# A finished background bank copied ahead of the fourth exp, second norms turned in other places, fewer background products in the attention's last steps

## The chip, the cores and the metric

The kernel runs on one core of a Trainium2 chip. The metric is the device time of one execution in microseconds (us), as a median of several runs; smaller is better. The five engines are named as the profile names them: PE is TensorE's matmul, PEld its weight load, DVE is VectorE, ACT is ScalarE, POOL is GpSimd, SP is SyncE, which here issues most DMAs. PSUM, into which TensorE writes, has eight banks, numbered 0 to 7 here. A bank holds 128x512 float32 values.

## The reference

A transformer block with adaptive layer norm, batch 1, 2048 rows, width 512, 32 heads of 16, FFN width 1792, all float32:

```
sa, ca, ga, sb, cb, gb = split(silu(c) @ w_mod)        # six vectors of 512
h = layernorm(x) * (1 + ca) + sa
q, k, v = heads(h @ wqkv)
o = softmax(q k^T / 4) v                                # 32 heads, 2048 x 2048 scores each
x = x + ga * (o @ wo)
h = layernorm(x) * (1 + cb) + sb                        # the second norm
x = x + gb * (gelu(h @ w1 + b1) @ w2 + b2)
```

The result must be near float32 accuracy. The kernel therefore splits most operands into a high and a low part and makes three products of each pair (high by high, low by high, high by low).

## The kernel before

**Blocks and units.** The rows are cut into four blocks of 512. A unit is one block of queries with four heads; there are 4x8 = 32 units, and 16 chunks of 128 keys in each, so 512 half-steps (`for hs in range(NU * NKC): half_step(hs)`). I call them steps, as the prediction does.

**What a step does** (`half_step`, L1026). For one unit and one chunk of keys: four score products `e` (`exp_mm`), each followed by an exp on ScalarE that writes a tile `p`; four products `mx` (`mx_mm`), whose row maxima VectorE takes for a unit that comes later (`LEAD` = 88 products ahead); and at its end the sums `pv` (`pv_step`) of the step before, four heads side by side. Score and maximum products use 64 of the array's rows each, so two of them on different row halves run together. PSUM is dealt out in rings: `e` has banks 0, 1, 2; `mx` has 3, 4, 5; `pv` has 6; `bg` has 7 alone.

**Background work.** Everything else of the model runs in the gaps of the steps: the projections of q, k, v, the attention's output product, the FFN. The generator `work()` yields jobs in order. A job is either a group (a list of products into one bank, and an `evac` that copies the finished bank out), a callable, or `None` (nothing to do yet). A step takes at most one new job and issues six products (`RUN = 6`) of the running group. These are cut to 64 rows as well, one half of the rows in even steps and the other in odd ones, so each pairs with an `e` or `mx` product on the other half. A group of 12 products is 24 such halves, four steps. When the group is complete, `bg_mm` calls `evac`, which puts a copy from bank 7 on ScalarE's queue. When the row halves change within a group, the first product waits for an instruction of another engine that proves the half before done; this is what the tiny copy `tick` (L1080) is for.

**The order inside a step.** With background work running, the step issues one `e` and one `mx`, then in the loop over `k` = 0 to 5 one background product and one `e` (`k` = 0, 2, 4) or `mx` (`k` = 1, 3, 5). Each exp follows its `e` at once in the order of issue, so the fourth exp (`k` = 4) stands on ScalarE ahead of the copy of a bank that gets complete at `k` = 5. Without background work the loop at the end of `half_step` issues pairs of `e` and `mx`, four times.

**The clock of the hooks.** Every exp calls `advance()`, which counts `clock["t"]` up by one and runs what was put there with `later(n, f)`. A step is four ticks. The two parts of the FFN's gelu, additions, statistics and stores are placed so. `sides` is a list of callables; each step runs one of them at its beginning. V's turns go there (`turn_v("mx")`, in a bank of the `mx` ring).

**The second norm** (`front`, L805). For a block `b`, four groups make the output product; each is copied (`y`), added to `x2[t]` on GpSimd, its statistics are taken on VectorE (`stat`), then the factor (`factor`), then the normalized rows `xn[t]` (`norm`, L818). When all four are there and nine ticks have gone by, four callables `trans(fc)` are yielded. Each takes the `bg` bank, transposes four 128x128 pieces of `xn` into it (L853), copies it out on ScalarE with scale and offset (`h`, L855), and GpSimd makes the high and the low part from it (L856, L857). A callable makes the step *full*: it runs at the step's beginning, and if the next job is a callable too, that one is held for the next step, so four steps have a turn and no background product. Blocks 1 and 2 start `front` ahead of the last part of the FFN of the block before (`"last"` in `work`), and their turns follow that part.

**The FFN** (`feed`, L863). `ffn1(i)` is a group of the first matrix; its `evac` starts the gelu: a copy `h` (L882), three GpSimd operations (L883 to L885), and with `later(10, second)` the tanh on ScalarE (L888) and four more GpSimd operations (L890 to L893). The second matrix follows in three parts (`PARTS`).

**The attention's end.** When all maxima are taken (from step 490 on), `ending` is set: the `e` ring gets banks 0 to 4, `bg` gets 5 and 7, and new groups run with all 128 rows, `RUN // 2` = 3 products in a step (`bg_whole`), behind that step's four `e` products. After the last step the running group is finished, `over[0]` is set, and the tail does what is left: from then on the gelu is one instruction (L875, L877, L878) and VectorE adds the FFN's sums. `o_prep` fetches the last unit's sums from DRAM, takes the reciprocal of the denominators (`dn`, L717), stores and loads it (`rden`, `rb`) and divides; its hooks also ask for weights (`wload`, L784). Then come the last block's output products (tile `o`), norm and FFN.

Of the kernel before, what the change touches and what calls it, by code (L numbers as in the profile page):

```python
# [23 lines left out]
KC = D // P  # L24
# [35 lines left out]
RUN = 6  # L60
# [9 lines left out]
def block_kernel(ctx: ExitStack, tc: tile.TileContext, x, wqkv, wo, w1, b1, w2, b2, c, w_mod, out):  # L70
# [179 lines left out]
    def later(n, f):  # L250
        if n:
            hooks.setdefault(clock["t"] + n, []).append(f)
        else:
            f()
# [550 lines left out]
    def front(b, x2):  # L805


        later(9, lambda: load_x2(b, x2))
        yield from until(lambda: done[b] == KC - 1)
        yield from wait(4)  # L810
        yield from loaded(b, *[("o", k) for k in range(KC)])
        mv = small.tile([P, 4, 2], F32, tag="mv", name="mv")
        rs = {}
        xn = {}

        def norm(t):
            xn[t] = tmp("xn")
            (gp if t < 3 else ve).tensor_scalar(  # L818
                xn[t], x2[t], mv[:, t, 0:1], rs[t], op0=ALU.subtract, op1=ALU.mult)
            later(40, lambda: gp.tensor_tensor(x2[t], x2[t], b2_b, op=ALU.add))  # L820

        def stat(t):
            ln_stat(mv, t, x2[t])
            later(2 if t < 3 else 1, lambda: factor(t))

        def factor(t):
            rs[t] = small.tile([P, 1], F32, tag=f"rt{t}", name=f"rt{t}")
            ve.tensor_scalar(rs[t], mv[:, t, 1:2], EPS, None, op0=ALU.add)  # L828
            gp.tensor_tensor(rs[t], rs[t], mhalf[:, 0:1], op=ALU.pow)
            later(3 if t < 3 else 2, lambda: norm(t))  # L830

        for t in range(4):

            def evac(ps, t=t):
                y = tmp("y")
                ac.activation(y, ps, AF.Copy)

                def add():
                    gp.tensor_tensor(x2[t], y, x2[t], op=ALU.add)
                    later(4 if t < 3 else 3, lambda: stat(t))  # L840

                later(2, add)

            yield o_terms(b, t, range(KC)), "bg", evac
        drop(b, *[("o", k) for k in range(KC)])
        t0 = clock["t"]
        yield "ln"
        yield from until(lambda: len(xn) == 4 and clock["t"] >= t0 + 9)

        def trans(fc):  # L850
            ps = take("bg")
            for t in range(4):
                te.transpose(ps[:, t * P : (t + 1) * P], xn[t][:, fc * P : (fc + 1) * P], ident)  # L853
            h = tmp("h32")
            ac.activation(h, ps, AF.Identity, scale=modc[:, 1, fc, 0:1], bias=modc[:, 1, fc, 1:2])  # L855
            gp.tensor_copy(pc(b, fc, 0), h)  # L856
            gp.tensor_tensor(pc(b, fc, 1), h, pc(b, fc, 0).bitcast(F32), op=ALU.subtract)  # L857

        for fc in range(KC):
            yield lambda fc=fc: trans(fc)  # L860
        yield from wait(4)

    def feed(b, x2):  # L863
# [7 lines left out]
        def ffn1(i):  # L871
            def evac(ps):
                h = tmp("h")
                if over[0]:
                    ac.activation(h, ps, AF.Gelu_apprx_tanh, bias=b1_f[0][:, i : i + 1])  # L875
                    g = piece(i)
                    ac.activation(g[:, 0], h, AF.Copy)  # L877
                    ve.tensor_tensor(g[:, 1], h, g[:, 0].bitcast(F32), op=ALU.subtract)  # L878
                    gt[i] = g, clock["t"] - 9
                    return  # L880
                s = tmp("s")
                ac.activation(h, ps, AF.Identity, scale=0.5, bias=b1_h[:, i : i + 1])  # L882
                gp.tensor_tensor(s, h, h, op=ALU.mult)  # L883
                gp.tensor_scalar(s, s, GELU_C, 1.0, op0=ALU.mult, op1=ALU.add)
                gp.tensor_tensor(s, s, h, op=ALU.mult)  # L885

                def second():
                    ac.activation(s, s, AF.Tanh, scale=2 * GELU_A)  # L888
                    g = piece(i)
                    gp.tensor_scalar(s, s, 1.0, None, op0=ALU.add)  # L890
                    gp.tensor_tensor(h, s, h, op=ALU.mult)
                    gp.tensor_copy(g[:, 0], h)
                    gp.tensor_tensor(g[:, 1], h, g[:, 0].bitcast(F32), op=ALU.subtract)  # L893
                    gt[i] = g, clock["t"]

                later(10, second)

            wi = wt[b, 1, i].rearrange("p a (k n) -> p a k n", n=P)
            k = range(KC)
            return terms3([wi[:, 0, j] for j in k], [wi[:, 1, j] for j in k],  # L900
                          [pc(b, j, 0) for j in k], [pc(b, j, 1) for j in k]), "bg", evac
# [124 lines left out]
    def half_step(hs):  # L1026
# [6 lines left out]
            wload()  # L1033
        if sides:
            sides.pop(0)()
        full = False
        if act["g"] is None:
            j = held.pop() if held else next(jobs, None)
            if callable(j):
                j()  # L1040
                full = True
                j = next(jobs, None)
            if callable(j):
                held.append(j)
            elif j is not None:
                act["g"] = {"group": j, "at": [0, 0], "n": 0, "seen": None, "whole": bool(ending)}
# [7 lines left out]
            return sum(ec) < ne and ec[a] < 2 * NU * NKC  # L1054

        more = act["g"] is not None
        free = not more and not full and not ending
        if more and act["g"]["whole"]:
            while sum(ec) < ne:
                for f in [exp_mm(a) for a in range(2) if e_ok(a)]:  # L1060
                    f()
            for _ in range(RUN // 2):
                if act["g"]:
                    bg_whole()
            more = False
        k = 0
        first = more and x_ok(1 - h) and e_ok(h)
        if first:
            for f in [exp_mm(h), mx_mm(1 - h)]:
                f()  # L1070
        while more and k < RUN:
            a = 1 - h
            more = bg_mm(h)
            if first:
                if e_ok(a) and (k % 2 == 0 if x_ok(a) else sum(ec) < ne - 1 or k == RUN - 1):
                    exp_mm(a)()
                elif x_ok(a):
                    f = mx_mm(a)
                    if more and k == RUN - 1:
                        saw(ve.tensor_copy(tick, mxb[0][:, :1]))  # L1080
                    f()
            elif e_ok(a) and (sum(ec) < ne - 1 and k % 2 == 1 or not x_ok(a) and (sum(ec) < ne - 1 or k == RUN - 1)):
                exp_mm(a)()
            elif x_ok(a):
                mx_mm(a)()
            k += 1
        while sum(ec) < ne or sum(xc) < nx:
            a = 0 if ec[0] <= ec[1] else 1
            fs = []
# [7 lines left out]
                fs += [mx_mm(i) for i in range(2) if x_ok(i)]  # L1097
            for f in fs:
                f()
        if hs:  # L1100
            assert min(ec) >= 2 * cur["pv"] + 2
            pv_step()

# [162 lines left out]
```

## Time and profile before

| what | value | where it is from |
|---|---|---|
| median of 3 runs | 1719.15 us (1718.91 to 1720.06) | the times |
| profiled execution, its own time | 1721.25 us | its result |
| span of the profiled execution | 1719.5 us, 32477 instructions | head of the page |
| granted TensorE clock | 0.996 of full speed | its result |
| steps: first and last `pv` | 113.4 and 1595.7 us | the row of L669 |
| DMA | 251.89 MB, mean 146 GB/s | part 2 of the page |

The profile holds one execution. The rows of its page and of the answers to queries name the source line (L644 is line 644), the engine, the operation, and the tiles as out<-in, with buffer numbers left out. A group's row gives busy time, the mean duration of one instruction, and the idle time of its engine ahead of it with what ended most of it. A timeline row gives start, length and the instruction; in brackets stands the idle time of the engine before it and what ended it. Matmul ends are modelled, so "PE busy" is not TensorE at its peak, and a wait of a few tenths can hide in it; the time from one matmul's start to the next one's is the better measure.

### The profile page before, as it was taken

To read this page: it belongs to the slowest core of one execution; us is meant where nothing else is said; L and a number is where in the kernel's file an instruction comes from. 1 tells how busy PE (TensorE), PEld (TensorE's weight loads), DVE (VectorE), ACT (ScalarE), POOL (GpSimd) and SP (SyncE) were. 2 spreads that over 40 slices of the span, in tenths; PEclk is the share of its full clock that TensorE was granted. 3 is DMA by queue.
4 is the path that set the end of the run, shared out by engine and by line. 5 is a ranking of instruction groups with operands and counts; after the bars stand their busy time and mean duration, and the time that the engine had idled before them with its cause. 6 is when DMAs were issued, how large, how long until landed. Compare 5 with 4: busy or idle time off the path is not lost.

```text
span 1719.5 us, 32477 instructions
## 1 busy us (share of the span) xinstructions
PE 1692.2 (98%) x12073; PEld 916.6 (53%) x12073; DVE 1400.8 (81%) x2661; ACT 1238.0 (72%) x2379; POOL 694.7 (40%) x703
## 2 busy tenths in 40 slices
PE   7999999999999999999999999999999999999999
PEld 6655555555554455555555455555555545553677
DVE  7998888888889888888989888888899888870332
ACT  3357878778777778778877788778877778878231
POOL 7324444435112356415623246415633246526310
PEclk8999999999999999999999999999999999999999
DMA  8646766767447533425453444345363354423554
GB/s 292 195 156 208 221 200 204 221 192 218 125 149 210 127 99 101 104 71 153 128 163 95 111 123 119 95 107 139 116 181 82 100 143 119 98 73 116 193 156 161
DMA packets 137129, 251.89 MB, mean 146 GB/s; under 512 B 25854, under 2 KB 45324, under 8 KB 136972
## 3 DMA queue, kind: packets, MB, share of 16 engines
q1 hardware_dynamic: 135712, 248.19, 50.2%
q8 instruction: 96, 1.57, 0.4%
q10 hardware_dynamic: 1260, 1.63, 0.3%
q14 instruction: 61, 0.50, 0.1%
HBM read 188.49 MB, written 61.28 MB: 145 GB/s over the span
## 4 chain that ended last, share of the span: by engine, by line
PE 88%; DVE 6%; DMA 3%; ACT 2%; issue 0%; POOL 0%; SPq 0%; ACTq 0%; DVEq 0%; POOLq 0%
PE bg L275 39%; PE pv L669 28%; PE e L639 15%; DVE mxp L394 4%; PE mx L389 3%; DMA w<-w1s 1%; ACT p L644 1%; DVE bst L236 1%; PE pr L275 1%; PE o L275 1%; DMA wt<-wos 0%; DMA wm<-in_w_mod_dram 0%; ACT h L855 0%; PE bg L853 0%; PE mx L334 0%
## 5 line engine op out<-in xcount | busy, mean ns | idle before, releaser
L394 DVE TENSOR_REDUCE mxp<-mx 128x1 f32<-128x512 f32 x2048 | 1294.0, 683 | 163.1 <-PE mx L389 155.3
L644 ACT ACTIVATE p<-e 128x512 f32<-128x512 f32 x2035 | 1057.6, 604 | 283.5 <-PE mx L389 262.4
L389 PE MATMUL mx<-kh,qst 48*128 48x512 f32 x2048 | 835.5, 422 | 2.3 <-DVE rt L828 0.6
L639 PE MATMUL e<-qst,kh 50*128 50x512 f32 x2035 | 777.1, 429 | 6.2 <-ACT p L644 6.2
L639 PEld LDWEIGHTS e<-qst,kh 50*128 50x128 f32 x2035 | 341.6, 185 | 426.1 <-ACT p L644 218.0
L669 PE MATMUL pv<-p,vg 128*32 128x512 f32 x4096 | 546.0, 605 | 0.0
L389 PEld LDWEIGHTS mx<-kh,qst 48*128 48x128 f32 x2048 | 369.4, 185 | 19.5 <-DVE mxp L394 14.1
L275 PE MATMUL bg<-w,g 64*128 64x512 f32 (+1 forms) x1056 | 267.5, 392 | 0.8 <-DVE tick L1080 0.8
L275 PEld LDWEIGHTS bg<-w,g 64*128 64x128 f32 (+1 forms) x1056 | 193.2, 185 | 36.2 <-ACT p L644 2.7
L669 PEld LDWEIGHTS pv<-p,vg 128*32 128x32 f32 x4096 | 80.9, 108 | 177.2 <-issue 165.1
L275 PE MATMUL bg<-pchi,w 64*128 64x512 f32 (+1 forms) x624 | 174.7, 398 | 0.0
L275 PE MATMUL bg<-hThi,wqkv 64*128 64x512 f32 x560 | 155.3, 396 | 0.2 <-DVE tick L1080 0.2
L275 PEld LDWEIGHTS bg<-pchi,w 64*128 64x128 f32 (+1 forms) x624 | 111.7, 185 | 26.4 <-ACT h L882 6.1
L890 POOL TENSOR_SCALAR s<-s 128x512 f32<-128x512 f32 x41 | 61.3, 1496 | 129.1 <-ACT s L888 129.0
L275 PEld LDWEIGHTS bg<-hThi,wqkv 64*128 64x128 f32 x560 | 101.1, 185 | 16.1 <-DVE tick L1080 0.5
L909 POOL TENSOR_TENSOR x<-y,x 128x512 f32<-128x512 f32 x28 | 36.1, 1288 | 148.9 <-ACT y L908 148.4
L275 PE MATMUL bg<-pclo,w 64*128 64x512 f32 (+1 forms) x312 | 85.0, 389 | 0.0
L878 DVE TENSOR_TENSOR g<-h,g 128x512 fp32r<-128x512 f32 x15 | 10.8, 723 | 83.6 <-ACT g L877 83.6
L275 PE MATMUL bg<-hTlo,wqkv 64*128 64x512 f32 x280 | 76.5, 392 | 0.0
L275 PEld LDWEIGHTS bg<-pclo,w 64*128 64x128 f32 (+1 forms) x312 | 57.1, 184 | 10.1 <-issue 2.1
L275 PE MATMUL bg<-wo,pchi 64*128 64x512 f32 x192 | 61.2, 398 | 1.3 <-DVE tick L1080 0.6
L883 POOL TENSOR_TENSOR s<-h 128x512 f32<-128x512 f32 x41 | 42.7, 1042 | 48.4 <-ACT h L882 48.4
(159 smaller groups left out, 1366.0 us busy)
## 6 DMA issues: line engine op xcount, KB each, us to landing
kh<-qk SPq DMA_DIRECT2D x256, 192.0 KB
w<-w1s SPq DMA_DIRECT2D x56, 512.0 KB
w<-w2s SPq DMA_DIRECT2D x54, 512.0 KB
vg<-v SPq DMA_DIRECT2D x64, 332.0 KB
qk<-parts SPq DMA_DIRECT2D x32, 512.0 KB
qst<-qk SPq DMA_DIRECT2D x64, 192.0 KB
qk<-parts SPq DMA_DIRECT2D x32, 256.0 KB
ou<-osb SPq DMA_DIRECT2D x32, 256.0 KB
```

The source lines that it names most:

```text
L236: ve.bn_stats(st, rows)
L275: return te.matmul(ps, term[0][r], term[1][r], start=i == 0, stop=i == n - 1)
L389: te.matmul(ps, qst[u][r0 : r0 + KR, p, qc * P : (qc + 1) * P], kh(u, kr // 2)[r0 : r0 + KR, p, (kr % 2) * TB : (kr % 2 + 1) * TB], start= ...
L394: ins = ve.tensor_reduce(mxp[u][:, hc, kr : kr + 1], ps, axis=AX.X, op=ALU.max, negate=True)
L639: te.matmul(ps, kh(u, kc // 8)[r0 : r0 + KX, p, (kc % 8) * P : (kc % 8 + 1) * P], qst[u][r0 : r0 + KX, p], start=True, stop=True)
L644: saw(ac.activation(t, ps, AF.Exp, scale=SCALE))
L669: te.matmul(cur["ps"][32 * j : 32 * (j + 1)], vg[u][:, kc, j * VW : j * VW + 32], pt.pop(4 * s + j), start=kc == 0, stop=kc == NKC - 1)
L878: ve.tensor_tensor(g[:, 1], h, g[:, 0].bitcast(F32), op=ALU.subtract)
L883: gp.tensor_tensor(s, h, h, op=ALU.mult)
L890: gp.tensor_scalar(s, s, 1.0, None, op0=ALU.add)
L909: later(4, lambda: gp.tensor_tensor(x2[t], y, x2[t], op=ALU.add))
```

## The change

Four things are edited.

1. In a step with background work, the `e` product at `k` = 4 is issued as before, but its exp is kept in `fourth` and issued only after the loop, behind a copy that `evac` may have issued at `k` = 5. The count of the clock moves with it. `later(10, second)` becomes `later(9, second)`.
2. In blocks 1 and 2 the second norm's turns are no longer jobs. When the fourth `xn` is there, nine ticks later four callables are put into `sides`, with a bank of the `mx` ring; each runs at the beginning of a step, ahead of that step's usual work. `front` ends when all four are done and eight ticks have passed.
3. In block 0 the turns are still jobs, but a step holds its callable in `turn` and runs it after the third of its four `e` products, where there is no background group; where there is one, at the beginning.
4. In the attention's last steps a step issues two background products where `hs % 3` is not zero, and three where it is.

```diff
@@ front: norm
             later(40, lambda: gp.tensor_tensor(x2[t], x2[t], b2_b, op=ALU.add))
+            if b and len(xn) == 4:
+                later(9, lambda: sides.extend([lambda fc=fc: trans(fc, "mx") for fc in range(KC)]))
...
         t0 = clock["t"]
-        yield "ln"
-        yield from until(lambda: len(xn) == 4 and clock["t"] >= t0 + 9)
-
-        def trans(fc):
-            ps = take("bg")
+
+        def trans(fc, bk="bg"):
+            ps = take(bk)
...
             gp.tensor_tensor(pc(b, fc, 1), h, pc(b, fc, 0).bitcast(F32), op=ALU.subtract)
-
+            turned[fc] = clock["t"]
+
+        turned = {}
+        yield "ln"
+        if b:
+            yield from until(lambda: len(turned) == KC and clock["t"] >= turned[KC - 1] + 8)
+            return
+        yield from until(lambda: len(xn) == 4 and clock["t"] >= t0 + 9)
         for fc in range(KC):
             yield lambda fc=fc: trans(fc)
@@ feed: ffn1
-                later(10, second)
+                later(9, second)
@@ half_step
-        full = False
+        full, turn = False, None
         if act["g"] is None:
             j = held.pop() if held else next(jobs, None)
             if callable(j):
-                j()
+                turn = j
                 full = True
                 j = next(jobs, None)
...
         more = act["g"] is not None
+        if more and turn:
+            turn()
+            turn = None
         free = not more and not full and not ending
...
-            for _ in range(RUN // 2):
+            for _ in range(2 if hs % 3 else 3):
                 if act["g"]:
                     bg_whole()
...
         first = more and x_ok(1 - h) and e_ok(h)
+        fourth = None
...
                 if e_ok(a) and (k % 2 == 0 if x_ok(a) else sum(ec) < ne - 1 or k == RUN - 1):
-                    exp_mm(a)()
+                    if k == RUN - 2:
+                        fourth = exp_mm(a)
+                    else:
+                        exp_mm(a)()
...
             k += 1
+        if fourth:
+            fourth()
         while sum(ec) < ne or sum(xc) < nx:
...
             for f in fs:
                 f()
+            if turn and sum(ec) == ne - 1:
+                turn()
+                turn = None
         if hs:
+            assert not turn
```

## The prediction

> **What bounds the kernel now.** I read the page first (busy shares, then the chain that ended last), then cut the middle of the run into half-steps: the time from one group of attention products (`pv`) to the next, 512 in all, called steps here.
>
> ```profile
> PE 1692.2 (98%) x12073; PEld 916.6 (53%) x12073; DVE 1400.8 (81%) x2661; ACT 1238.0 (72%) x2379; POOL 694.7 (40%) x703
> ...
> PE 88%; DVE 6%; DMA 3%; ACT 2%; issue 0%; POOL 0%; SPq 0%; ACTq 0%; DVEq 0%; POOLq 0%
> ```
>
> TensorE works almost always and is 88% of the chain, so each step's length is TensorE's, plus what makes its next product wait. The next rows are stages (from:to, length, then busy us and instructions of PE, PEld, DVE, ACT, POOL): the first and second step of a background group of the first FFN matrix, the first step of an attention-output group, and the third step of such a group.
>
> ```profile
> 685.88:688.86 2.98, 2.98 (x25) 1.43 (x23) 2.62 (x6) 2.78 (x6) 2.83 (x4) 1.00 0.60 177
> 688.86:691.70 2.84, 2.84 (x24) 1.49 (x22) 2.43 (x6) 1.93 (x5) 2.38 (x3) 1.00 0.60 137
> 898.36:901.26 2.90, 2.90 (x24) 1.46 (x22) 2.54 (x6) 2.61 (x6) 1.29 (x1) 1.00 0.69 247
> 904.11:907.31 3.20, 3.12 (x24) 1.58 (x23) 3.17 (x9) 2.78 (x7) 1.55 (x2) 1.00 0.19 70
> ```
>
> An undisturbed step takes 2.84. A group's first step takes 0.14 more in the FFN case and 0.06 in the other. The timeline at such a border shows why.
>
> ```profile
> 673.03 2.07 ACT L644 ACTIVATE p<-e 128x512 f32<-128x512 f32 x4 [0.27 <-PE mx L389]
> ...
> 673.97 0.39 PE L275 MATMUL bg<-pclo,w 64*128 64x512 f32 x1
> ...
> 674.34 1.07 PE L669 MATMUL pv<-p,vg 128*32 128x512 f32 x8
> 674.81 0.61 POOL L892 CAST g<-h 128x512 fp32r<-128x512 f32 x1
> 674.96 0.71 ACT L882 ACTIVATE h<-bg,b_h 128x512 f32<-128x512 f32 x1
> ...
> 675.72 0.18 PEld L275 LDWEIGHTS bg<-pchi,w 64*128 64x128 f32 x1 [0.20 <-ACT h L882]
> ...
> 676.07 0.19 PEld L639 LDWEIGHTS e<-qst,kh 50*128 50x128 f32 x1
> ```
>
> The group's last product is done at 673.97+0.39 = 674.36, but ScalarE's copy `h` of the only background bank (7) begins at 674.96, behind four exps (2.07/4 = 0.52 each). The next group's first weight load waits 0.20 for that copy, and what follows on TensorE slips.
>
> **The change, part by part.**
>
> (a) *Copy ahead of the fourth exp.* The order of ScalarE alone changes; no instruction is added. Three exps end at 673.03+3×0.52 = 674.58, after the last product (674.36), so the copy need not wait for TensorE: it would run from 674.58 to 675.29, 0.43 before the load that waits until 675.72. Behind it on ScalarE stands the fourth exp, 675.29 to 675.81. Two things wait for that: the `pv` of the next step, 2.84 later, and the `e` bank that the next step's third score product takes (three banks in turn), whose load is at 676.07 here and about 0.14 earlier, 675.93, in an undelayed step. So the exp is covered by 0.12. How often it counts: ScalarE's copies out of that bank in the main loop.
>
> ```profile
> L882 ACT ACTIVATE h<-bg,b_h x36: 712/712/717, 617.4 to 1477.0; 128x512 f32<-128x512 f32 x36
> L908 ACT ACTIVATE y<-bg x27: 628/628/629, 715.4 to 1528.5; 128x512 f32<-128x512 f32 x27
> L309 ACT ACTIVATE pf<-bg x23: 628/628/688, 119.8 to 519.7; 128x512 f32<-128x512 f32 x23
> L644 ACT ACTIVATE p<-bg x13: 616/616/628, 522.1 to 1276.3; 128x512 f32<-128x512 f32 x13
> L323 ACT ACTIVATE vr<-bg x12: 628/628/673, 131.3 to 380.8; 128x512 f32<-128x512 f32 x12
> L836 ACT ACTIVATE y<-bg x12: 628/628/641, 547.6 to 1324.0; 128x512 f32<-128x512 f32 x12
> L855 ACT ACTIVATE h<-bg,modc x12: 777/778/779, 593.1 to 1382.5; 128x512 f32<-128x512 f32 x12
> ```
>
> 36 borders with the long copy at 0.14 = 5.0; the 74 others (27+23+12+12, all 0.628 long) at 0.06 = 4.4. Together **-9.4**; bounds 0 (the exp's cover is used up and gives it back) and -10.5. The clock of the hooks counts exps, so everything timed from a copy now comes one tick earlier. The tanh, with `later(9)` in place of 10, is issued behind the fourth exp of the second step, where ScalarE is at 1.93 of 2.84; I cost it at nothing. Uncovered (were GpSimd late with its input) it would hold the next exps. The second norm's statistics on VectorE also move a tick: they stand in the twelve 3.20 steps (DVE 3.17), 0.36 over. I take 0; if the earlier place hides them -4.3, if it doubles them +4.3.
>
> (b, c) *Turns.* The rows: a step that only turns (block 0), a step with neither turn nor background, a step with background and a turn of V beside it, and the first two of block 1's four turn steps.
>
> ```profile
> 601.85:605.35 3.50, 2.99 (x22) 1.25 (x20) 2.48 (x5) 2.73 (x7) 1.90 (x3) 1.00 0.00 0
> 881.27:884.01 2.74, 2.64 (x18) 1.01 (x17) 2.38 (x5) 2.46 (x6) 0.49 (x1) 1.00 0.98 236
> 173.04:176.59 3.55, 3.55 (x29) 1.93 (x27) 2.65 (x6) 2.60 (x7) 0.00 (x0) 1.00 0.23 59
> 980.42:984.22 3.80, 3.06 (x22) 1.25 (x20) 2.97 (x8) 2.99 (x7) 1.28 (x4) 1.00 0.20 44
> 984.22:987.72 3.50, 2.97 (x23) 1.26 (x21) 2.48 (x5) 2.73 (x7) 3.12 (x4) 1.00 0.83 204
> ```
>
> (b) Block 0: its four turns go from the head of an otherwise empty step to a place behind the third exp. At the head TensorE idles 3.50-2.99 = 0.51, since the exps wait behind the norm's copy (0.78). Behind the third exp that copy delays only the fourth. What TensorE needs: a full step less the three pairs that six background products make, at 0.23 each (the `o` row below: 9.82/42), plus a turn, 3.55-2.84 = 0.71, so 2.84-0.70+0.71 = 2.85; ScalarE needs 2.73, VectorE 2.48. I take 2.90: 4×(3.50-2.90) = **-2.4**; bounds -3.0 (2.74, all in slack) and 0. GpSimd's cast and subtract (1.90) come along, under 2.90. No DMA moves with a turn.
>
> The Trainium skill, TensorEngine Tiling (Array Packing), section Tiling Modes, says that changing the tiling mode drains TensorE. Inside the step the 128-row turn stands between 64-row pairs, so it adds one switch that the head position did not have. The row nearest to a switch is the border above: from the last product (673.97) to `pv` (674.34) are 0.37 where pairs follow at 0.23, so 0.14 by estimate, and (b) would be -1.8; the trace agrees as far as that goes.
>
> (c) Blocks 1 and 2: the eight turns go into steps that also carry background, as V's do, in a maximum bank instead of bank 7. From V's 3.55, plus 0.15 because the norm's copy is one of 0.78 ahead of four exps: 3.70 each. Eight such steps are 29.6; the eight that they replace were 2×(3.80+3×3.50) = 28.6. So **+1.0** in the loop (bounds 0 and +6.8, 4.43 each with the price doubled), but the eight now carry 48 half products, 24 whole ones, two groups, that are no longer left for the end.
>
> (d) *The end.*
>
> ```profile
> 1568.03:1570.58 2.55, 2.55 (x17) 0.94 (x16) 0.00 (x0) 2.06 (x5) 2.38 (x4) 1.00 0.39 153
> 1549.97:1593.80 43.83, 43.83 (x256) 16.47 (x255) 0.00 (x0) 39.24 (x78) 28.79 (x27) 1.00 0.31 102
> 1596.30:1617.15 20.85, 19.45 (x81) 14.82 (x81) 5.79 (x10) 4.41 (x6) 10.64 (x11) 1.00 0.58 198
> ```
>
> When the maxima are used up, 19 steps carry three whole products each: 57. Seventeen of them take 43.83, 2.58 each, with TensorE full. Groups start at step 493 as before (eight turn steps are two whole groups), and 493 mod 3 is 1, so a group of 12 now takes 2, 2, 3, 2, 2 and 1: six steps, 2.0 on average, 38 products in 19 steps. One product less is 0.23, so 2.35; ScalarE needs 39.24/17 = 2.31 with a copy and a tanh every fourth step, less with one every sixth. I take 2.37: 19×(2.58-2.37) = **-4.0**, bounds -1 and -4.4.
>
> (e) *The tail.* From the copy of the last attention bank (1596.30) to the dense output products it is 20.85. The chain there:
>
> ```profile
> 1604.01 0.06 DVE g L878
> 1604.07 0.55 issue
> 1604.61 0.36 DVE dn L717
> ...
> 1608.54 8.57 DMA wt<-wos
> 1617.11 0.04 issue
> 1617.15 9.82 PE o L275 x42
> ```
>
> The reciprocal `dn` stands on VectorE behind `g` of the last FFN group, and the weights `wos` are asked for only behind it. Left over after the loop are 75 background products (15 of the first matrix, 60 of the second; with the first six output products they are the 81 of the last row above); now 75-24+19 = 70. The last first-matrix group is then already under way, takes the GpSimd path, and leaves VectorE free: `dn` stands behind one addition, after 10+12 products, 22×0.23 = 5.1 and about 0.9, so 6.0 behind 1596.30 instead of 8.3. TensorE itself needs 70×0.23 = 16.1. Between 16.1 and 20.85 I take 18.0, near the chain's 20.85-2.3: **-2.9**.
>
> Sum: -9.4-2.4+1.0-4.0-2.9 = **-17.7**. The profiled execution took 1721.25, its span 1719.5; they would become 1703.6 and 1701.8. The median shown, 1719.15, lies 2.1 below the profiled time, and gives **1701.5**.
>
> **The rivals.**
>
> *The copy ahead gives nothing back.* What it frees at a group's first product it loses at the next step's third score product. For it: a cover of only 0.12. Against: ScalarE's 2.78 of 2.98 leaves room. Then -8.3: 1710.9.
>
> *Turns beside sums cost double* because the borrowed maximum bank holds up the maxima: +5.8 over the sum, 1707.3. For it: three such banks only. Against: V's turns do the same at 3.55.
>
> *The tail keeps its 20.85*, since `wos` is bound by its 8.57 of transfer and not by `dn`: 1704.4.
>
> *Slower.* At each border the fourth exp ends later than the 0.12 of cover, the third score product and all behind it slip. At 0.25 lost per border, 110×0.25 = +27.5, with the other terms' -8.3: +19, 1738. It decides from 0.08 lost per border (8.3/110). For it: the copy now waits for the last background product, and the exp behind it. Against: that product ends 0.22 before the third exp.
>
> The Trainium skill, TensorE: Matmul & The Clock Gate, Part 1, calls ScalarE strict FIFO, so the exp can't pass a waiting copy. The rows agree so far: `h` started only after four exps.
>
> **How the numbers follow.** Forecast 0.60, own range 1697 to 1706; nothing from the copy 0.12; dear turns 0.10; tail unchanged 0.13; slower 0.05. The range 1696 to 1711 leaves out the slower case, half of the first rival and the forecast's edges, about 2 in 10. What a measurement tells from no change is 0.2%, 3.4 us: all cases but the slower one are beyond it; I leave 0.03 for losses that cancel. Faster 0.92, same 0.03, slower 0.05.
>
> **What would show it.** (a) First steps of groups at 2.84 to 2.86, copies of `bg` between third and fourth exp, and no wait of background loads for them. (b) Block 0's four turn steps near 2.9. (c) Block 1's and 2's near 3.7, with six background products in each. (d) Last steps near 2.35, 38 products in them. (e) `dn` about 6 behind the last bank's copy, `o` at about 18. It would be wrong if steps within groups, not at their borders, changed: longer second or third steps would mean that the moved tanh or statistics hold ScalarE or VectorE.

## The result and the profile after

The changed kernel takes **1706.82 us** (median of 4 runs, 1705.32 to 1709.14), the kernel before 1719.61 (4 runs, 1718.91 to 1721.08). The ratio is 0.9926, with a 95% interval of 0.9909 to 0.9943: 12.8 us less, where the prediction has 17.7 less.

The page of the changed kernel, part 1 (busy time) and part 4 (chain that ended last):

```profile
PE 1685.2 (99%) x12097; PEld 921.8 (54%) x12097; DVE 1400.8 (82%) x2666; ACT 1235.7 (73%) x2379; POOL 702.2 (41%) x710
...
PE 93%; DVE 4%; DMA 2%; POOL 0%; ACT 0%; issue 0%; SPq 0%; POOLq 0%; DVEq 0%; ACTq 0%
```

TensorE was 88% of the chain and is 93% now; ScalarE's 2% is gone. The bound is the same engine, waited for less.

Four stages tell where the time went. The cuts are the first sums `pv`, those of step 488 (where the maxima run out), those of step 511, and the end. Columns: from:to, length, then busy us and instructions of PE, PEld, DVE, ACT and POOL, granted clock, DMA share, GB/s. First the kernel before:

```profile
0.00:113.42 113.42, 102.40 (x525) 70.67 (x526) 99.61 (x174) 38.90 (x67) 55.49 (x64) 0.94 0.71 227
113.42:1536.91 1423.49, 1412.84 (x10685) 729.50 (x10683) 1260.24 (x2420) 1121.52 (x2176) 585.80 (x588) 1.00 0.50 139
1536.91:1594.76 57.85, 57.78 (x349) 22.10 (x348) 1.95 (x5) 50.25 (x99) 30.99 (x31) 1.00 0.37 118
1594.76:1719.50 124.74, 119.17 (x523) 94.31 (x519) 39.04 (x64) 27.36 (x41) 22.45 (x21) 1.00 0.52 175
```

and the changed kernel:

```profile
0.00:110.56 110.56, 99.61 (x526) 68.38 (x526) 99.42 (x174) 38.88 (x67) 55.50 (x64) 0.97 0.74 233
110.56:1525.83 1415.27, 1413.48 (x10733) 740.69 (x10731) 1258.13 (x2426) 1120.80 (x2178) 589.62 (x592) 1.00 0.51 141
1525.83:1579.99 54.16, 54.04 (x330) 19.32 (x329) 1.95 (x5) 49.49 (x98) 33.22 (x33) 1.00 0.29 88
1579.99:1703.40 123.41, 118.07 (x518) 93.38 (x514) 41.35 (x63) 26.53 (x40) 23.91 (x23) 1.00 0.51 177
```

The loop is 8.2 shorter, the ending 3.7, the tail 1.3: together 13.2, near the medians' 12.8. The start is 2.9 shorter too, but the change doesn't touch it: in the traces of all kernels here it lies between 110.6 and 114.0 with the same work. It is scatter of single executions, so kernels are compared below by the three later stages and by medians. In the loop TensorE ran 48 matmuls more than before (10733 for 10685: the 24 products, in halves, that moved forward) in less time, and what it lost beside its busy time fell from 10.7 (1423.49-1412.84) to 1.8.

Single steps of the changed kernel: the first step of a first-matrix group; block 0's turn; a turn beside sums; the second step of an output group (with the second norm's statistics); then the first and the third step of a projection group.

```profile
679.82:682.67 2.85, 2.85 (x25) 1.48 (x23) 2.49 (x5) 2.64 (x6) 2.33 (x4) 1.00 0.57 172
588.23:591.14 2.91, 2.91 (x21) 1.25 (x21) 2.65 (x6) 2.12 (x5) 0.00 (x0) 1.00 1.08 267
937.97:941.70 3.73, 3.73 (x29) 1.96 (x27) 2.78 (x6) 3.22 (x7) 1.05 (x2) 1.00 0.01 3
893.69:896.85 3.16, 3.16 (x24) 1.65 (x23) 3.12 (x8) 2.39 (x6) 0.00 (x0) 1.00 0.00 0
306.13:309.04 2.91, 2.91 (x25) 1.51 (x23) 2.55 (x6) 2.57 (x6) 2.02 (x3) 1.00 0.46 149
311.89:314.80 2.91, 2.91 (x25) 1.51 (x23) 2.60 (x6) 2.06 (x5) 0.00 (x0) 1.00 1.01 237
```

The first row was 2.98 before, the second 3.50, the third stands for 3.80 or 3.50. The last two are taken up in point (a) below. The timeline at the border of that first row:

```profile
678.50 1.57 ACT L644 ACTIVATE p<-e 128x512 f32<-128x512 f32 x3 [0.77 <-PE mx L389]
...
679.45 0.39 PE L275 MATMUL bg<-pclo,w 64*128 64x512 f32 x1
...
679.82 1.06 PE L669 MATMUL pv<-p,vg 128*32 128x512 f32 x8
...
679.94 0.70 ACT L889 ACTIVATE h<-bg,b_h 128x512 f32<-128x512 f32 x1
...
680.51 0.62 ACT L644 ACTIVATE p<-e 128x512 f32<-128x512 f32 x1
...
680.92 0.19 PEld L639 LDWEIGHTS e<-qst,kh 50*128 50x128 f32 x1
...
681.16 0.39 PE L639 MATMUL e<-qst,kh 50*128 50x512 f32 x1
...
681.39 0.19 PEld L639 LDWEIGHTS e<-qst,kh 50*128 50x128 f32 x1
```

Three exps, the copy `h` 0.10 behind the end of the last product (679.45+0.39), then the fourth exp, as the prediction had it. No background load waits for `h`. The exp ends at 681.13, and the next step's third score product loads at 681.39: a cover of 0.26.

### The profile page after: what moved, and what is told of

It is laid out like the page before. It is cut to its first block, busy times and chain, and to the rows that moved or that the text cites. A ratio compares the mean times of both kernels' runs of the same rounds, so it can differ in the third digit from the quotient of the medians.

```text
span 1703.4 us, 32435 instructions
## 1 busy us (share of the span) xinstructions
PE 1685.2 (99%) x12097; PEld 921.8 (54%) x12097; DVE 1400.8 (82%) x2666; ACT 1235.7 (73%) x2379; POOL 702.2 (41%) x710
## 3 DMA queue, kind: packets, MB, share of 16 engines
q8 instruction: 96, 1.57, 0.4%
## 4 chain that ended last, share of the span: by engine, by line
PE 93%; DVE 4%; DMA 2%; POOL 0%; ACT 0%; issue 0%; SPq 0%; POOLq 0%; DVEq 0%; ACTq 0%
PE bg L275 40%; PE pv L669 30%; PE e L639 16%; PE mx L389 4%; DVE mxp L394 3%; PE pr L275 1%; PE o L275 1%; DMA wt<-wos 0%; DMA wm<-in_w_mod_dram 0%; PE mx L334 0%; DVE bst L236 0%; DMA qst<-qk 0%; PE mx L853 0%; DMA wraw<-in_A_wqkv_dram 0%; DVE hTlo L483 0%
## 5 line engine op out<-in xcount | busy, mean ns | idle before, releaser
L639 PEld LDWEIGHTS e<-qst,kh 50*128 50x128 f32 x2035 | 334.1, 185 | 421.9 <-issue 214.5
L389 PEld LDWEIGHTS mx<-kh,qst 48*128 48x128 f32 x2048 | 370.2, 185 | 22.8 <-DVE mxp L394 17.7
L275 PEld LDWEIGHTS bg<-w,g 64*128 64x128 f32 (+1 forms) x1056 | 195.5, 186 | 29.8 <-POOL m L411 0.2
L275 PEld LDWEIGHTS bg<-pchi,w 64*128 64x128 f32 (+1 forms) x640 | 117.3, 185 | 23.0 <-issue 5.5
L410 POOL CAST m<-mt 128x32 fp32r<-128x32 f32 x32 | 6.7, 210 | 120.1 <-DVE mt L408 115.4
```

The costliest lines, as they stand in the source:

```text
L275: return te.matmul(ps, term[0][r], term[1][r], start=i == 0, stop=i == n - 1)
L389: te.matmul(ps, qst[u][r0 : r0 + KR, p, qc * P : (qc + 1) * P], kh(u, kr // 2)[r0 : r0 + KR, p, (kr % 2) * TB : (kr % 2 + 1) * TB], start= ...
L410: gp.tensor_copy(m2[:, 0], mt)
L639: te.matmul(ps, kh(u, kc // 8)[r0 : r0 + KX, p, (kc % 8) * P : (kc % 8 + 1) * P], qst[u][r0 : r0 + KX, p], start=True, stop=True)
```

## The experiments

The theory: the time falls only where TensorE no longer waits (borders, block 0's turns) or gets work where it would have waited; a background product costs it 0.23 wherever it runs. The rivals: the moved products are the gain themselves; the exp's cover is all but used up; the tail hangs on one late item (reciprocal, weights or GpSimd's gelu). Ratios are to the kernel before, with the 95% interval; edits are to the changed kernel but for the first.

**The copy alone.** The kernel before with the fourth exp behind the copy and `later(9, second)`, nothing else:

```diff
-                    exp_mm(a)()
+                    if k == RUN - 2:
+                        fourth = exp_mm(a)
+                    else:
+                        exp_mm(a)()
...
+        if fourth:
+            fourth()
```

> The kernel before with nothing but the fourth exp issued behind the copy and the tanh's hook at 9. Theory (the copy's place at the border of two background groups was the cost): the steps that begin a group fall to 2.84 in the groups of the first FFN matrix (2.97 before) and by about 0.05 in the others; 8 us in all, 1711 to 1713 where the kernel before takes 1719.6, a good half of the whole change. Rival (the other edits make the gain, the exp that now waits gives it back): within 2 us of the kernel before.

1713.26 (1711.93 to 1714.37), ratio 0.9959 (0.9944 to 0.9974). Its loop:

```profile
113.62:1530.43 1416.81, 1408.34 (x10684) 735.38 (x10682) 1259.53 (x2420) 1119.55 (x2176) 586.33 (x588) 1.00 0.50 139
```

1423.49 became 1416.81: the copy is worth 6.7, the ending stays at 57.9, and the tail goes from 124.7 to 124.0.

**A shorter cover.** The third exp is issued behind the copy as well:

```diff
-                    if k == RUN - 2:
-                        fourth = exp_mm(a)
+                    if k == RUN - 2 or k == RUN - 4 and sum(xc) < 64 * NU - 8:
+                        late.append(exp_mm(a))
...
-        if fourth:
-            fourth()
+        for f in late:
+            f()
```

> The changed kernel, but the third exp too is issued behind the copy, as the fourth is. Theory of the cover: the copy then waits for the last background product, the third exp ends at about 1.2 behind pv's start, and the next step's second score product, which takes that exp's bank and is loaded 1.1 behind pv, waits: each border loses 0.2 to 0.3, 110 borders, so 20 to 35 us slower than the changed kernel (1727 to 1742). Rival (ScalarE has room enough, the place among the exps does not matter as long as the copy is early): within 3 us of the changed kernel's 1706.8.

1716.01 (1712.89 to 1717.11, 10 runs), ratio 0.9975 (0.9965 to 0.9984): 9.2 over the change, so neither forecast came out. Its loop, and its row and timeline at the border shown above:

```profile
113.96:1537.41 1423.45, 1421.48 (x10733) 752.78 (x10731) 1260.26 (x2426) 1122.92 (x2178) 589.38 (x591) 1.00 0.50 140
...
684.92:687.85 2.93, 2.93 (x24) 1.64 (x22) 2.58 (x6) 2.87 (x6) 2.02 (x4) 1.00 0.55 184
```

```profile
684.92 1.06 PE L669 MATMUL pv<-p,vg 128*32 128x512 f32 x8
...
686.21 0.18 PEld L639 LDWEIGHTS e<-qst,kh 50*128 50x128 f32 x1
...
686.25 0.45 PE L639 MATMUL e<-qst,kh 50*128 50x512 f32 x1
...
686.69 0.18 PEld L639 LDWEIGHTS e<-qst,kh 50*128 50x128 f32 x1
```

The loop gives back 8.2 over some 110 borders, 0.07 each on average, and this border 0.08 (2.93 for 2.85). The rivals' mechanism is real, but cheap. The second score product loads 1.29 behind `pv` instead of 1.10 (680.92-679.82), 0.19 later; its product still starts 1.33 behind, where it was 1.34. In the change the load runs 0.24 ahead of its product (681.16-680.92), and here that lead took up the delay. The third load, which needs the fourth exp's bank, is 0.20 later as well (1.77 behind `pv` for 1.57); what is left of all that by the end of the step is the 0.08.

**The turns in empty steps.** Blocks 1 and 2 turn as block 0 does, behind the third score product of steps without background work:

```diff
-            if b and len(xn) == 4:
-                later(9, lambda: sides.extend([lambda fc=fc: trans(fc, "mx") for fc in range(KC)]))
...
-        if b:
-            yield from until(lambda: len(turned) == KC and clock["t"] >= turned[KC - 1] + 8)
-            return
```

> The changed kernel, but the second norms of blocks 1 and 2 are turned as block 0's are: behind the third score product of steps without background work. Theory (a turn beside background work costs 3.73 where one in an empty step costs 2.91): the eight steps fall from 29.8 to 23.3, 6.5 less; 24 products are left for the end, where the tail waits anyway until its weights land, so only about 2.4 of their 5.5 come back: 4 us faster than the changed kernel, 1702 to 1704. Rival (work is only moved): the 5.5 come back in full, within 1.5 us of 1706.8.

1708.23 (1706.61 to 1709.13), ratio 0.9929 (0.9914 to 0.9944), the same as the change: the rival came out, the work is only moved. Its loop and its tail:

```profile
113.68:1523.61 1409.93, 1407.60 (x10684) 735.74 (x10682) 1259.49 (x2420) 1119.46 (x2176) 586.45 (x588) 1.00 0.51 140
...
1577.75:1707.00 129.25, 123.27 (x542) 97.97 (x538) 40.49 (x65) 29.07 (x44) 25.22 (x23) 1.00 0.51 177
```

The loop is 5.3 shorter, near the 24 products that it no longer carries (5.5 at 0.23), and the tail is 5.8 longer.

**Three products at the end.** Edit (d) taken back:

```diff
-            for _ in range(2 if hs % 3 else 3):
+            for _ in range(RUN // 2):
```

> The changed kernel with three products in each of the attention's last steps, as before. 19 products fewer are then left for the tail. Theory (the tail's first 20 us are set by its chain of transfers, so products left for it are hidden): the last 23 steps take 57.9 instead of 54.2 and the tail keeps its 123.4, so 3.7 slower than the changed kernel, about 1711. Rival (the tail is TensorE's, the 19 products come off it again): the tail shrinks by 19 x 0.23 = 4.4, within 1 us of the changed kernel.

1709.85 (1709.54 to 1711.86), ratio 0.9941 (0.9926 to 0.9956): 3.0 over the change by the medians, whose intervals overlap, and 3.3 by the three stages of the traces. Its ending and its tail, and from the chain what comes ahead of the dense output products:

```profile
1529.28:1587.22 57.94, 57.84 (x348) 22.10 (x347) 1.95 (x5) 51.28 (x101) 43.31 (x42) 1.00 0.32 100
1587.22:1709.70 122.48, 114.57 (x499) 91.12 (x495) 38.18 (x62) 25.43 (x38) 15.56 (x15) 0.98 0.49 170
```

```profile
1594.11 4.47 DMA rden<-dn
...
1599.79 6.24 DMA wt<-wos
...
1606.08 11.39 PE o L275 x42
```

The ending takes back its 3.8, and the tail is only 0.9 shorter, though 19 products (4.4 us) left it. From `osb` (1588.81) to the dense output products are 17.3 us, in which TensorE is busy for 13.5: with 51 products the chain of reciprocal and weights binds, with 70 TensorE is busy for 18.3 of 19.6. So (d) gains, beside the change's turns, because its products fill a wait.

**Both together.** Empty turns for all blocks and three products at the end: the two edits above at once:

```diff
-            for _ in range(2 if hs % 3 else 3):
+            for _ in range(RUN // 2):
...
-        if b:
-            yield from until(lambda: len(turned) == KC and clock["t"] >= turned[KC - 1] + 8)
-            return
```

> The changed kernel with the second norm's turns of blocks 1 and 2 behind the third score product of empty steps, as block 0's, and with three background products in each of the attention's last steps, as before the change. Theory (a background product costs TensorE 0.23 us wherever it runs, and the time falls only where a wait goes): the loop loses 5.3 us as in the run with empty turns alone (1409.9), the ending takes its 19 products back (57.9), and the tail is left with 75 products as in the run of the copy alone (about 124, output products dense at 20.0): together 1.0 to 1.5 us below the changed kernel, ratio to the kernel before 0.992. Rival (the second matrix's weights come late because of the order of the work and not because of the number of products left): the tail stays at 129.3 and the ending is dearer all the same, ratio 0.995.

1706.11 (1705.26 to 1706.87, 5 runs), ratio 0.9920 (0.9907 to 0.9934). Loop, ending and tail:

```profile
111.61:1521.67 1410.06, 1407.74 (x10685) 735.95 (x10683) 1259.57 (x2420) 1119.46 (x2176) 586.52 (x588) 1.00 0.51 140
1521.67:1579.58 57.91, 57.82 (x348) 22.14 (x348) 1.94 (x5) 50.26 (x99) 31.49 (x31) 1.00 0.36 118
1579.58:1703.50 123.92, 118.92 (x523) 94.37 (x519) 39.07 (x64) 27.34 (x41) 21.97 (x21) 1.00 0.51 176
```

All three stages came out as the theory's sum has them, and the rival's tail of 129 did not. As fast as the change, within the intervals, without turns beside sums and without fewer products at the end: only the copy and the place of the turns inside the step are needed for the gain. With the turns in empty steps edit (d) gains nothing: 1708.23 with it, 1706.11 without. From the copy alone (1713.26) the twelve turns are worth some 7, 0.6 each.

**The tail's late item: gelu.** The group that is under way when the attention ends is finished behind the switch to the short gelu, so that GpSimd's path is not taken:

```diff
-    while act["g"]:
-        bg_whole() if act["g"]["whole"] else bg_mm(hs % 2)
...
+    while act["g"]:
+        bg_whole()
```

> The changed kernel, but the last group of the first FFN matrix that is under way when the attention ends takes the short gelu path (one ScalarE function, subtract on VectorE) in place of the seven operations with GpSimd. Theory (in the changed kernel the load of the inverted denominators, rb, is issued 3.3 us after their store instead of 1.45, because its buffer is still read by GpSimd's gelu of the group before, which stands behind the last group's): rb is issued 1.5 to 2 earlier, the output weights land earlier, the dense output products begin 17.5 to 18 behind the last bank's copy instead of 19.55; 1.5 to 2 us faster, 1705. Rival (the weights' transfer is the bound by itself): output products at 19.5, no change.

1708.59 (1707.19 to 1709.57), ratio 0.9932 (0.9916 to 0.9949): its tail of 123.4 is the change's own. TensorE no longer waits for GpSimd there (0.68 in the change), but for weights instead, and GpSimd's path alone is not what holds the tail.

**The tail's late item: weights.** All six pieces asked for on ScalarE's queue at once:

```diff
-    def wload():
+    def wload(q=sy):
...
-        sy.dma_start(t.bitcast(F32), {"o": wo_d, 1: w1_d, 2: w2_d}[key[1]][key[2]])
+        q.dma_start(t.bitcast(F32), {"o": wo_d, 1: w1_d, 2: w2_d}[key[1]][key[2]])
...
+    for _ in range(6):
+        wload(ac)
```

> The changed kernel, but six weight tiles (the rest of the second matrix and the four of the output product) are asked for on ScalarE's DMA queue as soon as the attention has ended, instead of behind the load of the inverted denominators. Theory (after the attention the dense output products wait only for these weights, whose 2 MB share the transfer rate with what is asked for at the same time): they land in the first 10 us, the dense output products begin 16.3 to 17.5 behind the last bank's copy instead of 19.55, which is TensorE's own 70 products; the tail falls from 123.4 to about 121, 2 to 3 us faster than the changed kernel. Rival (the chain of the denominators is the bound, or is slowed by the weights): 19.5 or later, no gain.

1717.36 (1716.12 to 1719.68, 10 runs), ratio 0.9984 (0.9974 to 0.9993): the tail is 133.1, 9.6 longer. Its chain of waits and ScalarE's timeline:

```profile
1587.66 10.53 DMA ob<-ou
...
1598.21 0.33 ACTq L784
```

```profile
1587.26 11.76 ACTq L784 DMA_DIRECT2D wt<-wos  x4
1599.07 1.15 ACT L895 ACTIVATE s<-s 128x512 f32<-128x512 f32 x2 [12.14 <-DMA w<-w1s]
```

The four `wos` requests stood on ScalarE's queue for 11.76, and the tanh behind them began 12.1 late (its row names a weight load as what ended that wait; on its own engine it stood behind the requests). It is not the issuing that took this time, 0.33 to 0.54 a request: by the semaphores in the trace the second request waited for the landing of the first `w2s` (1590.54), and the third, at 1598.21, for that of the load `ob` (1587.66+10.53 = 1598.19). GpSimd's gelu came late, and TensorE waited for its `g`. That load `ob` of the last unit's sums took 10.5 beside the weights, 5.3 in the change. The Trainium skill, DMA: Bandwidth & Descriptors, section Issuing engines are not separate DMA queues, says that DMAs of all engines interleave on the same 16 DMA engines and a second issuer saves sequencer time only. The trace agrees (10.5 for 5.3); what it adds is the price for the issuer's own work, 12.1, when its requests have to wait.

**The tail's late item: when `wos` is asked for.** Four pieces at the store of the reciprocal instead of one:

```diff
             if over[0]:
-                wload()
+                for _ in range(4):
+                    wload()
```

> The changed kernel, but after the attention four weight tiles (what is left of the second matrix, then output weights) are asked for while the inverted denominators are being stored, ahead of their load on SyncE's queue, instead of one; nothing is moved to another queue. Theory (the dense output products wait for 3 MB that are asked for only when the denominators' load has been issued, while the transfer engines are half idle for the 3 us before): the output weights land 2 to 2.5 earlier, the products begin 17.3 to 17.8 behind the last bank's copy instead of 19.55, the tail falls from 123.4 to 121 to 121.5; 1705 beside the changed kernel's 1707. Rival (the denominators' load is then late instead, behind the weights): the fourth part of the output product waits for it, no gain.

1706.70 (1706.11 to 1707.08, 5 runs), ratio 0.9919 (0.9905 to 0.9932). `osb` to dense output products is 18.8 instead of 19.6 and the tail 122.75 instead of 123.41; the whole can't be told from the change. With the gelu's edit on top (both diffs as above):

```diff
+                for _ in range(4):
+                    wload()
...
+    while act["g"]:
+        bg_whole()
```

> The kernel of wos_ahead with the short gelu path of short_gelu. Theory: with the weights no longer the bound, the denominators' load comes 0.5 earlier and the last sums of the FFN do not wait for GpSimd: 0.5 to 1 faster than wos_ahead. Rival: the same as wos_ahead within 0.5 in the tail.

1710.55 (1709.79 to 1711.43), ratio 0.9943 (0.9928 to 0.9958), tail 125.8, so the two do not add. With five pieces and the turns in empty steps:

```diff
+                for _ in range(5):
+                    wload()
...
-        if b:
-            yield from until(lambda: len(turned) == KC and clock["t"] >= turned[KC - 1] + 8)
-            return
```

> The kernel with all second norms turned in empty steps (empty_turns), and five weight tiles asked for ahead of the denominators' load. Theory (there the tail began its output products at 24.75 although TensorE's 94 products need only 21.6, because weights came late): they begin at 22 to 23, the tail falls from 129.3 to 127 or less, 1705 to 1706. Rival (the last tiles wait for slots that free only as products are done): 24.5, no gain over 1708.

1713.64 (1712.04 to 1714.40), ratio 0.9957 (0.9945 to 0.9970). The tail is 135.0, 5.7 longer than with empty turns alone. The five pieces (four of the second matrix and one of the output product, in the order of `stream`) did not repair that tail, and its timeline shows what they held up:

```profile
1598.35 0.69 DVE L736 TENSOR_TENSOR ob<-ob,rb 128x512 f32<-128x512 f32 x1 [10.18 <-DMA rb<-rden]
...
1600.93 5.46 PE L275 MATMUL bg<-wt,g 128*128 128x512 f32 x12 [5.33 <-issue]
```

The load `rb`, asked for behind them, landed 21.5 behind `osb`, where it took 16.5 with empty turns alone. VectorE stood at the division that needs it, the additions that empty the FFN's banks stood behind the division, and TensorE waited 5.33 for such a bank, where it had waited 0.93.

**The statistics.** The second norm's statistics one tick earlier for the first three rows:

```diff
-                    later(4 if t < 3 else 3, lambda: stat(t))
+                    later(3, lambda: stat(t))
```

> The changed kernel with the second norm's statistics one tick earlier for the first three of four row tiles: they are then issued behind the fourth exp of a step, after VectorE's last maximum of that step. Theory (the statistics stand ahead of a step's first maximum, so the banks of the maxima come free late and the step takes 3.05 to 3.15 in place of 2.84; behind the last maximum they run while TensorE does the sums): the second steps of the output groups fall from 3.05 to under 2.95, 1 to 2.5 us faster than the changed kernel. Rival (VectorE is late wherever they stand): the excess only moves to another step, no gain.

1706.43 (1705.72 to 1708.01), ratio 0.9920 (0.9905 to 0.9935). The same step as in the change's row 893.69:896.85:

```profile
896.96:900.12 3.16, 3.16 (x27) 1.66 (x28) 3.13 (x8) 2.39 (x6) 0.38 (x1) 1.00 0.00 0
```

It has VectorE full at 3.13 all the same: maxima and statistics together exceed a step, so the place of the statistics matters little.

**The tanh.** `later(9, second)` back to 10:

```diff
-                later(9, second)
+                later(10, second)
```

> The changed kernel with the tanh's hook at 10 as before: one exp later, behind the first exp of a group's third step instead of behind the fourth of its second. Theory (ScalarE is idle at the head of a step for 0.8, and the tanh of 0.63 only fits there): the third steps of the first matrix's groups rise from 2.85 by 0.05 to 0.15, 2 to 5 us slower than the changed kernel. Rival (ScalarE's slack covers it anywhere): third steps unchanged, within 1 us.

1709.68 (1708.62 to 1711.05), ratio 0.9940 (0.9923 to 0.9956); the intervals overlap. The third steps of first-matrix groups take 2.85 in both, so the tanh costs nothing in either place. Its loop is 1.5 longer, 1.2 of it in one step (windows, then SyncE's waits there):

```profile
1216.86:1221.45 4.59, 3.25 (x25) 1.54 (x23) 3.29 (x6) 2.93 (x7) 3.10 (x3) 1.00 0.32 79
```

```profile
SPq L727 <- DMA rden<-dn: 4.1, 1, 4.1
```

SyncE stood 4.1 for the store `rden`, and the loads behind it on its queue came late. The same step takes 3.35 in the change and 3.06 before. Whether the hook brings that about or it scatters is left open.

## Why the prediction was right or wrong

The direction, the loop's mechanisms and their order of size were right, and 1706.8 lies inside the range; it lies 0.8 above the forecast's own range, because two terms of the sum were too big.

**(a) The copy: mechanism right, term too big (6.7 for 9.4).** The step that failed is "the 74 others (27+23+12+12, all 0.628 long) at 0.06 = 4.4": they gave 2.3. 35 of those copies are projections, and they gained 0.2 in all. The 0.06 is not a price of their border. In the kernel before, a first step of a projection group and the third step of the next one's, where no bank is copied:

```profile
308.91:311.82 2.91, 2.91 (x24) 1.49 (x22) 2.54 (x5) 2.55 (x6) 1.54 (x3) 1.00 0.52 175
...
314.66:317.55 2.89, 2.89 (x24) 1.51 (x23) 2.60 (x7) 2.06 (x5) 0.00 (x0) 1.00 0.96 228
```

Both are over 2.84, and the change's two rows of the same steps (2.91, 2.91) are not shorter. What costs every other projection step its 0.06 stays open. Over the loop of the copy-alone run, from the starts of `pv`: the first steps of the 36 first-matrix groups went from a mean of 2.996 to 2.866 (-4.7, near the prediction's 5.0). Five of them keep 0.16 to 0.18, with the copy `osb` of the attention's sums on ScalarE; the border in the prediction's timeline, at 674.34, is one of these. The first steps of the 27 second-matrix groups gave -1.7 in all (0.6 of it in two that carry a turn), those of the 12 output groups -0.4, of the 35 projections -0.2, the statistics' steps -0.4, and all other steps took 0.7 longer: together the -6.7.

The cover of 0.12, on which the slower rival rested, was 0.26. With a second exp behind the copy, which uses up more than that, a border lost 0.07 to 0.08 and not 0.25; that is near the 0.08 from which the prediction let that rival decide.

The Trainium skill, TensorE: Matmul & The Clock Gate, Part 2, section Step-by-step: what each phase is for, says that TensorE pulls weight loads ahead of matmuls that are under way. The trace agrees (0.24 ahead), and it bears on the rival: with two exps behind the copy a load was 0.19 late, and its product was not.

**(b) Block 0's turns: right.** Predicted 2.90 for 3.50; measured 2.92, 2.90, 2.91, 2.91. That is -2.3, near the -2.4 predicted. By the Trainium skill, TensorEngine Tiling (Array Packing), section Tiling Modes, the prediction had -1.8 for a drain at the added switch; above the 2.85 that TensorE's products need there are 0.06 and not 0.14, so the row speaks for less than that rule's estimate.

**(c) Turns beside sums: right.** 3.70 predicted, 3.72 to 3.74 measured; eight take 29.8 where the eight before took 28.6, +1.3 for +1.0. The rival with the doubled price fell. What the prediction did not see is that the 24 products so moved gain nothing: by the run with empty turns the loop without them is 5.3 shorter and the tail 5.8 longer.

**(d) The ending: right in size.** Seventeen of its steps:

```profile
1538.46:1579.02 40.56, 40.56 (x240) 14.04 (x239) 0.00 (x0) 38.19 (x76) 23.50 (x22) 1.00 0.19 61
```

2.39 each, where 2.37 was predicted and 2.58 stood before; the ending is 3.7 shorter (predicted 4.0). That this is a gain and not a move rests on the tail, as three products at the end show.

**(e) The tail: half of its term (1.3 for 2.9).** `osb` to dense output products became 19.6 (1581.58 to 1601.13), not 18.0. Two steps failed. The first is the floor, "TensorE itself needs 70×0.23 = 16.1". It leaves out the six output products that the prediction counts into its 81. The changed kernel's stretch:

```profile
1581.58:1601.14 19.56, 18.31 (x77) 13.84 (x77) 7.50 (x9) 2.44 (x4) 12.99 (x13) 1.00 0.57 215
```

With 76 products (the 77th is the first dense one) TensorE is busy for 18.31, as the prediction's own row has it (19.45 for 81, 0.24 each): 18.0 lay below that. Of the 1.3 by which this stretch got shorter, 1.1 is TensorE's work, five products fewer, and only 0.15 is waiting (20.85-19.45 = 1.40, 19.56-18.31 = 1.25).

The second step that failed is "near the chain's 20.85-2.3". The reciprocal did come early. The changed kernel's timeline:

```profile
1587.41 0.34 DVE L717 RECIPROCAL dn<-dn 128x32 f32<-128x32 f32 x1
1587.78 0.32 SPq L721 DMA_DIRECT2D rden<-dn  x1
...
1591.06 0.60 SPq L727 DMA_DIRECT2D rb<-rden  x1
```

SyncE's wait ahead of `rb`, and the chain behind it:

```profile
SPq L727 <- DMA rden<-dn: 2.4, 1, 2.4
```

```profile
1593.15 7.94 DMA wt<-wos
...
1601.13 9.81 PE o L275 x42
```

`dn` is 5.8 behind `osb`, as predicted (6.0; before 8.3). But the load `rb`, behind which the weights `wos` are asked for, follows the store `rden` by 3.3, where it was 1.45 before. In eleven of the fourteen kernels `rb` goes out 9.0 to 10.1 behind `osb`, whether `dn` is at 4.9 or at 8.3: the prediction let the chain move with its first link, and a later link did not move.

The trace has the times at which the parts of a transfer land, and they point to that link. All times here are counted from `osb`. In the changed kernel the store is issued at 6.20, and twelve of its sixteen parts land by 7.60. The last four land at 8.43, 8.88, 9.12 and 9.42, each 0.18 or 0.19 behind one of the last four parts of the load `ob` of the unit's sums (8.25, 8.70, 8.93, 9.23), and `rb` goes out at 9.48. With the short gelu the store's last four land at 8.75 to 8.93, 0.17 or 0.18 behind the load's, and `rb` goes out at 8.98; with three products at the end they land at 9.30 to 9.77, 0.18 to 0.23 behind, and `rb` goes out at 9.82. In the kernel before, the store was issued at 8.64, when that load was all but done (8.73), and landed whole by 10.04. So by these times the end of the early store comes behind the load `ob`, which doesn't hang on `dn`; no run moved that load alone. GpSimd's `h`, which the chain names ahead of `rb`, ended 0.12 after the request had begun, and the request took its usual 0.60.

The rivals: the copy did give something; turns beside sums were not dear; nothing was slower. The tail's rival was half right: 19.6 lies nearer to its 20.85 than to 18.0, but not for its reason, the transfer, since TensorE was busy for most of that time. That 1706.8 lies next to the 1707.3 of the dear turns is chance: their steps of 4.43 did not occur. The result is the forecast with (a) 2.7 and (e) 1.6 too big, 0.3 each in (c) and (d).

## What to carry to other kernels

Where one engine is the bound, work moved from stage to stage costs it the same everywhere: count a gain only for a wait that goes or one that gets filled. Before a small excess is put down to a border and multiplied, compare it with a step of the same kind that has no border. When the first link of a chain comes earlier, find the next link that does not hang on it before the whole chain is moved, and count all the work of the bound engine in that stretch: it is the floor.

## What the runs showed of the hardware

- A score product's weight load ran 0.24 ahead of the product, and at the border shown a load 0.19 late cost that product nothing and the step 0.08.
- Weight requests on ScalarE's queue held its next activation for 12.1 us, because one of them waited for the landing of a load from another queue; SyncE, too, stood 4.1 for one store of 16 KB.
- The 16 KB store of the reciprocal landed 1.40 behind its issue when the load ahead of it was done, and 3.2 behind it when issued 2.3 after that load: its last four parts followed that load's last four by 0.18 or 0.19.
- The first 110 us scattered by up to 3.4 us between executions of the same work (110.6 to 114.0), with a granted clock of 0.94 to 0.98 there, so that single profiled executions can't be compared by their whole span when a few microseconds are at stake.
